# Attention and squared-ReLU MLP on one core: down products in halves, outputs half a chunk later, background steps interleaved, x loaded ahead

## The chip, the cores and the metric

The kernel runs on one core of one Trainium2 chip. The metric is the device time of one launch in microseconds (us). The kernel before took a median of 578.99 us over 3 runs (578.84, 578.99, 581.28). The profiled execution took 579.12 us; its span, from the first to the last instruction of the trace, is 577.3 us, so 1.8 us lie outside the span.

## The reference, cut to what matters

```python
x: (4, 12480, 128)   inducing: (32, 128)   w_in: (128, 2048)   w_out: (2048, 128)

def mab(q, kv):
    s = scale * (q @ kv.transpose(0, 2, 1))
    s = s - s.max(-1, keepdims=True)
    a = np.exp(s)
    a /= a.sum(-1, keepdims=True) + 1e-09
    return a @ kv
h = mab(I, x)               # 32 rows of summary per batch, over all 12480 tokens
y = mab(x, h)               # every token attends to the 32 rows
r = np.maximum(y @ w_in, 0.0)
out = (r * r) @ w_out
```

Four batches of 12480 tokens pass through two attentions and then through an MLP with squared ReLU. In the second attention each token's row is a mixture of only 32 rows of `h`, with weights `a`.

## The kernel before, in words

**What is computed instead of the wide MLP.** Since y = a·h, a hidden unit is a·(h·w_in). Where such a unit keeps its sign over all tokens, its squared ReLU is a quadratic form in the 32 weights. The kernel writes that form with squares of differences of two weights: one product with the constant 0/1/-1 matrix `pairs` gives 512 values per token (`hp`, four blocks of 128), their squares are `g`, and a product with 512x128 weights `w16` plus a product with `lin` gives the output (`po`). `w16`, `lin` and what scales them belong to a batch and are worked out from `h`, `w_in` and `w_out`. A few units without a fixed sign go through rows 96 to 127 of the input tile `dT` (`sq`, `z`, `zz`). A flag tells whether the form holds; the general path behind it (from `all_columns` on) is not executed here.

**Stages of a batch** b, with 26 chunks of 480 tokens (120 tokens of each of four quarters), in 7 groups G of four chunks, the last one of two:
- `first(b)`: per group, load x transposed (`xp`, 9 buffers), scores `s` on TensorE, scaling and row maximum into `sT` on VectorE (L254). Then the global maximum (`m1`, `mt`, `gm`, `mb`, `nb`), per group exp on ScalarE (L300), a transpose into `en` (L310), `largest(G)`: the largest |x| of the group in one pass over up to 1920 columns (`xm`, L292), and 15 products with rows of x (`xnb`, 5 buffers) that are added up in `hq` (`hacc`, L323 and L331). Then `hs`, `hn`, `ht` and `hT`, the transposed summary.
- `prepare(b)`: `hwv` = h·w_in (16 products; copied out of PSUM by `evac`, L163), the bounds (`am`, `bc`, `two`), `hws` and its f16 form `hw16` (L497), `hwS`, `R`, `pl`, `rb`, `cat`, `w4`, and four times a table `G` (L605) whose 16 products `wq` give a block of `w16` (L165).
- `second(b, G)`: the scores of the second attention, exp, division by the sum (GpSimd does the subtraction and the multiplication), a transpose, a split into two f16 parts `a16`, out to DRAM (`ad`) and back as rows 0 to 95 of `dT`.
- `squares(b, G)`: `sq` on TensorE, `z` on VectorE, `zz` on GpSimd, four DMAs into rows 96 to 127 of `dT`.

**The main loop** runs over 104 chunks in two halves j. In each half ScalarE squares two blocks of `hp` into `g` (`lift`, L648, `g` has 3 buffers), TensorE writes the two blocks of the next chunk (`up`, L639, two PSUM slots). In the first half TensorE also does all five products of the chunk before (`down`: four of L654 and one of L655, two PSUM slots), the output `o` is scaled by ScalarE (L658) or VectorE (L660, `o` has 3 buffers) and its DMA is issued. After that `background(k)` writes whatever steps of the other stages are due: `second` runs two to three groups ahead, `first` and `prepare` of the next batch are spread over the 26 chunks, and `squares` runs a group ahead.

**What sets the order.** The generators give the order in which the program is written, and a step is what lies between two `yield`s. A scheduler then orders each engine's instructions by its own estimates, with the order of writing as the priority; each engine executes its list in order. Which engine takes an `o` or the high part of `a16` is decided by `to_act` from running sums of estimates. All DMAs are issued by one queue, SP's, in one order; GpSimd issues none.

**Before the main loop** a prologue turns the 64-bit words of the weights into f32 on VectorE (`narrow`), with `first(0)` between (at the steps named in `WHEN`), then `prepare(0)`. The first `g` starts at 100.27 us.

## Time and profile before

| what | value |
|---|---|
| median of 3 runs | 578.99 us |
| profiled execution, its span | 579.12 us, 577.3 us |
| mean granted TensorE clock | 0.869 |
| TensorE busy | 438.9 us (76%) |
| VectorE busy | 365.3 us (63%) |
| ScalarE busy | 296.8 us (51%) |
| GpSimd busy | 83.4 us (14%) |
| first `g` of the four batches | 100.3, 236.7, 360.8, 486.6 us |
| busy share of the 16 DMA engines by the hardware queue | 52.1% |

The busy shares are means over stages with different limits; the views by window, by group of instructions and by wait are read for each stage. "Idle before" in a group is the time that its engine stood still directly before these instructions, with what ended most of it. PE is TensorE's matmuls, PEld its weight loads, DVE VectorE, ACT ScalarE, POOL GpSimd and SPq the queue that issues the DMAs.

### The profile page before, as it was taken

How to read it: one execution, taken by the hardware profiler on the slowest of the kernel's cores; microseconds unless marked ns; L12 is line 12 of the kernel's file. 1: busy time of each engine (PE TensorE's matmuls, PEld its weight loads, DVE VectorE, ACT ScalarE, POOL GpSimd, SP SyncE). 2: the span in 40 equal slices, each digit the busy share in tenths (PEclk: the TensorE clock that was granted, in tenths of full speed). 3: DMA queues.
4: the chain of work that ended last, by engine and by line, in shares of the span. 5: the costliest groups of instructions: out<-in, count | busy, mean ns of one | idle time of the engine just before them, and what ended most of it. 6: DMA issues, size and time to landing. Idle time of an engine off the chain costs nothing.

```text
span 577.3 us, 8820 instructions
## 1 busy us (share of the span) xinstructions
PE 438.9 (76%) x3083; PEld 204.5 (35%) x3083; DVE 365.3 (63%) x947; ACT 296.8 (51%) x419; POOL 83.4 (14%) x93
## 2 busy tenths in 40 slices
PE   1615465777798889769878899769777999897882
PEld 0014334522233536413333545313243555223330
DVE  6999758662555268997254298985534378767342
ACT  0030112437577266747875376628574476565771
POOL 0000011030211010242021021222011022422010
PEclk9999655997789569989889799969969599899997
DMA  8958715024528606565867535735866332334543
GB/s 322 399 214 277 277 69 154 1 86 155 179 80 305 199 20 226 172 182 167 280 226 230 178 102 186 270 104 145 311 211 190 107 105 72 97 126 130 168 132 131
DMA packets 64590, 100.82 MB, mean 175 GB/s; under 512 B 22800, under 2 KB 53776, under 8 KB 64528
## 3 DMA queue, kind: packets, MB, share of 16 engines
q1 hardware_dynamic: 64528, 100.08, 52.1%
q8 instruction: 28, 0.46, 0.3%
q14 instruction: 34, 0.28, 0.2%
HBM read 64.91 MB, written 31.95 MB: 168 GB/s over the span
## 4 chain that ended last, share of the span: by engine, by line
PE 44%; DVE 28%; ACT 13%; issue 6%; DMA 3%; POOL 3%; SPq 1%; POOLq 0%; ACTq 0%; DVEq 0%
PE po L654 10%; PE hp L639 9%; ACT g L648 8%; PE s L236 7%; DVE xm L292 5%; PE hwv L448 5%; PE hacc L323 4%; DVE G L605 3%; DMA outT_dram<-o 2%; PE po L655 2%; PE wq L611 2%; ACT o L658 2%; DVE e L362 2%; PE R L529 2%; DVE z L372 2%
## 5 line engine op out<-in xcount | busy, mean ns | idle before, releaser
L648 ACT ACTIVATE g<-hp 128x960 f16<-128x960 f32 x208 | 193.2, 970 | 87.9 <-PE hp L639 48.9
L639 PE MATMUL hp<-dT,pairs 96*128 96x480 f16 x416 | 122.0, 385 | 29.0 <-ACT g L648 28.1
L654 PE MATMUL po<-g,w 128*128 128x480 f16 x416 | 119.4, 399 | 16.1 <-ACT o L658 6.0
L368 POOL TENSOR_TENSOR e<-e,mx 128x480 f32<-128x480 f32 (+1 forms) x28 | 26.5, 947 | 334.8 <-DVE mx L364 222.8
L639 PEld LDWEIGHTS <-pairs 96*128 96x128 f16 x416 | 37.8, 99 | 97.6 <-issue 75.7
L654 PEld LDWEIGHTS <-w 128*128 128x128 f16 x416 | 41.1, 104 | 75.4 <-issue 43.9
L292 DVE TENSOR_REDUCE xm<-xp_False 128x1 f32<-128x1920 f32 (+1 forms) x28 | 55.7, 1989 | 5.3 <-DMA xp_False<-xT_dram 5.3
L658 ACT ACTIVATE o<-po,bias,osc 128x480 f32<-128x480 f32 x66 | 48.9, 753 | 18.9 <-PE po L655 7.1
L236 PE MATMUL s<-xp_False,indT_sb 128*32 128x480 f32 (+1 forms) x224 | 37.7, 743 | 20.5 <-DMA xp_False<-xT_dram 12.3
L323 PE MATMUL hacc<-xnb,en 128*32 128x128 f32 x784 | 39.2, 328 | 17.2 <-issue 9.3
L655 PE MATMUL po<-dT,lin 128*128 128x480 f16 x104 | 42.3, 408 | 2.7 <-DMA dT<-zz 2.7
L432 POOL TENSOR_TENSOR zz<-z 128x480 f16<-128x480 f32 (+1 forms) x28 | 28.9, 1030 | 87.8 <-DVE z L428 72.1
L660 DVE TENSOR_SCALAR o<-po,osc,bias 128x480 f32<-128x480 f32 x38 | 28.7, 767 | 18.0 <-DMA outT_dram<-o 6.8
L323 PEld LDWEIGHTS hacc<-xnb,en 128*32 128x32 f32 x784 | 26.7, 129 | 34.3 <-issue 20.1
L300 ACT ACTIVATE sT<-sT,nb 128x480 f32<-128x480 f32 (+1 forms) x28 | 18.2, 653 | 35.5 <-DVE nb L287 35.5
L236 PE MATMUL s<-xp_False,hT 128*32 128x480 f32 (+1 forms) x224 | 34.5, 628 | 2.1 <-DVE s L357 1.7
L375 POOL TENSOR_TENSOR e<-e,z 128x480 f32<-128x480 f32 (+1 forms) x28 | 27.6, 986 | 53.8 <-DVE z L374 48.6
L428 DVE TENSOR_SCALAR z<-sq,off,cut 128x480 f32<-128x480 f32 (+1 forms) x28 | 21.4, 764 | 21.8 <-PE sq L422 21.7
L605 DVE TENSOR_TENSOR G<-hwp,hw 128x512 f16<-128x512 f16 x64 | 30.1, 510 | 5.0 <-PE wq L611 4.7
L369 ACT ACTIVATE e<-e 128x480 f32<-128x480 f32 (+1 forms) x28 | 16.1, 574 | 31.6 <-POOL e L368 31.6
L362 DVE STREAM_TRANSPOSE e<-s 128x480 f32<-128x480 f32 (+1 forms) x28 | 18.0, 644 | 15.4 <-PE s L236 14.9
L331 DVE TENSOR_TENSOR hq<-hacc,hq 128x128 f32<-128x128 f32 x24 | 6.8, 284 | 33.0 <-PE hacc L323 33.0
(208 smaller groups left out, 498.6 us busy)
## 6 DMA issues: line engine op xcount, KB each, us to landing
outT_dram<-o SPq DMA_DIRECT2D x104, 240.0 KB, 2.2
xp_False<-xT_dram SPq DMA_DIRECT2D x24, 960.0 KB, 5.8
xnb<-xn_dram SPq DMA_DIRECT2D x28, 448.0 KB, 6.1
xnb<-xn_dram SPq DMA_DIRECT2D x24, 512.0 KB, 5.8
dT<-ad SPq DMA_DIRECT2D x72, 120.0 KB, 2.7
ad<-a SPq DMA_DIRECT2D x24, 240.0 KB, 2.7
dT<-zz SPq DMA_DIRECT2D x104, 30.0 KB, 1.9
wi<-w_in_dram SPq DMA_DIRECT2D x4, 512.0 KB, 5.4
```

Source lines behind the costliest of these rows:

```text
L236: nc.tensor.matmul(ps[32 * q:32 * q + 32, 0:w], lhsT, xp[:, w * q:w * q + w], start=True, stop=True,)
L292: nc.vector.tensor_reduce(st.xm[:, G:G + 1], st.xp[G], axis=AX.X, op=ALU.max, apply_absolute_value=True,)
L323: st.last = nc.tensor.matmul(hacc[32 * q:32 * q + 32, 0:P], en[:, t], xg[:, t % 8], start=t < 4, stop=t + 4 >= nb32,)
L362: nc.vector.transpose(ef[:, 0:wb], ps[:, 0:wb])
L432: nc.gpsimd.tensor_tensor(g[rows], zv[rows], zv[rows], op=ALU.mult)
L448: nc.tensor.matmul(ps[:, k * (MI + 1):(k + 1) * (MI + 1)], w_in_sb[:, f:f + P], st.hT[:, 96:P + 1], start=True, stop=True,)
L605: tt(g[:, :, MI * j:MI * j + n], hwp[:, :, 0:n], hw16f[:, :, s0:s0 + n], op=ALU.mult)
L639: nc.tensor.matmul(hp[:, i, 0:CH].rearrange("p (q t) -> p q t", q=4), pairs[0:96, (2 * j + i) * P:(2 * j + i + 1) * P], self.dT[0:96], sta ...
L648: nc.scalar.activation(self.g[:, 2 * j:2 * j + 2], self.hp.pop(j)[:, 0:2, 0:CH], AF.Square)
L654: nc.tensor.matmul(po[:, 0:CH], st.w16[:, i], self.g[:, i], start=i == 0, stop=False)
L655: nc.tensor.matmul(po[:, 0:CH].rearrange("p (q t) -> p q t", q=4), st.lin, self.dT, start=False, stop=True)
L658: nc.scalar.activation(o, po[:, 0:CH], AF.Identity, bias=st.bias, scale=st.osc)
```

## The change

What it does, part by part:

1. `down` takes a half: products 0 and 1 are written in the first half of the next chunk, products 2 and 3 and the one with `lin` in its second half. The output of chunk n-2 is written as a function of its own, `out`, after the first lift of chunk n; that is half a chunk later than before.
2. `background` returns the list of due steps instead of doing them; the lists of `second`, of the next batch and of `squares` are interleaved one by one, and every other step is written ahead of the down products, the rest behind. `second` has two more `yield`s (between the subtraction and exp, and behind the transpose `a32`), and the step counts follow it.
3. `first` asks for three groups of `xp` before it starts and for one more per group; two of the row blocks `xnb` are asked for at group 4, three at the last group; before, `xp` was asked for a step ahead of its group and all five `xnb` behind the last group. `WHEN` is (0, 2, 4, 8, 10, 11, 12).
4. `largest` takes half a group per pass; the transpose `en` and exp of the next group are written ahead of these passes.
5. The copies of `hwv`, the two f16 copies `hw16` and the scaling of `w16` go from ScalarE (in the case of `hwv` and `w16`: from the choice of `evac`, which the profile shows on ScalarE each time) to VectorE. `cs` is copied a step sooner, the two copies into `g4` are behind a `yield`.

All calls on TensorE, ScalarE and VectorE go through a wrapper (`pe`, `act`, `dve`) that changes nothing, since `KEPT` is empty; in the listings of the changed program these instructions all carry its line, L75. The diff without the lines that only take the wrapper's name:

```diff
-WHEN = (0, 2, 4, 8, 10, 12, 14)
+LEAD = 3
+KEPT = ()
+WHEN = (0, 2, 4, 8, 10, 11, 12)
...
-        one.xm = const.tile([P, NG], F32, name=f"xm{k}")
+        one.xm = const.tile([P, 2 * NG], F32, name=f"xm{k}")
...
-        for G, w in enumerate(WID):
-            if b:
-                st.xp[G] = load_xT(b, G)
-                yield
...
-        xns = {h: load_xn(h) for h in range(XB)}
+        if b:
+            for G in range(LEAD):
+                st.xp[G] = load_xT(b, G)
+            yield
+        xns = {}
+        for G, w in enumerate(WID):
+            if b and G + LEAD < NG:
+                st.xp[G + LEAD] = load_xT(b, G + LEAD)
+            if G == NG - LEAD or G == NG - 1:
+                for h in range(XB):
+                    if (h < 2) == (G < NG - 1):
+                        xns[h] = load_xn(h)
...
-        def largest(G):
-            held["dve"] += 60 + 1.042 * 4 * WID[G]
+        def largest(G, k):
+            held["dve"] += 60 + 1.042 * 2 * WID[G]
+            dve.tensor_reduce(
+                st.xm[:, 2 * G + k:2 * G + k + 1], st.xp[G][:, 2 * k * WID[G]:2 * (k + 1) * WID[G]], axis=AX.X, op=ALU.max,
+                apply_absolute_value=True,
...
+        ens = {0: turned(0)}
+        largest(0, 0)
+        yield
+        for G, nb32 in enumerate(BLK):
+            en = ens.pop(G)
...
+            else:
+                ens[G + 1] = turned(G + 1)
+            largest(G, 1)
+            if G + 1 < NG:
+                largest(G + 1, 0)
             yield
...
         nc.gpsimd.tensor_tensor(e[:, 0:t], e[:, 0:t], mx[:, 0:t].unsqueeze(2).broadcast_to([P, t, MI]), op=ALU.subtract)
+        yield
...
-            evac(hwv[:, 8 * h:8 * h + 8].rearrange("p k i -> p (k i)"), ps[:, 0:8 * (MI + 1)], 8 * (MI + 1))
+            dve.tensor_copy(hwv[:, 8 * h:8 * h + 8].rearrange("p k i -> p (k i)"), ps[:, 0:8 * (MI + 1)])
...
-            nc.scalar.copy(hw16[:, :, k], hws)
+            dve.tensor_copy(hw16[:, :, k], hws)
...
-            evac(st.w16[:, c], ps[:, 0:P], P, tsg[:, c:c + 1])
+            ts(st.w16[:, c], ps[:, 0:P], tsg[:, c:c + 1], None, op0=ALU.mult)
...
-        def down(self):
+        def down(self, part):
             st = self.st
+            if part == 0:
+                self.po = ps_o.tile([P, 512], F32, tag="po", name=f"po_{self.b}_{self.c}")
+            po = self.po
+            for i in (2 * part, 2 * part + 1):
+                pe.matmul(po[:, 0:CH], st.w16[:, i], self.g[:, i], start=i == 0, stop=False)
+            if part == 0:
+                return
+            pe.matmul(po[:, 0:CH].rearrange("p (q t) -> p q t", q=4), st.lin, self.dT, start=False, stop=True)
...
-    N_SECOND, N_SCORES, N_HEADS, N_PRE, N_SQ = 4, 2 * NG, 20, 23, 2
+    N_SECOND, N_SCORES, N_HEADS, N_PRE, N_SQ = 6, NG + 1, 14, 23, 2
...
+        steps = []
+        while any(lists):
+            steps += [one.pop(0) for one in lists if one]
+        return steps
...
+            k += 1
+            steps = background(k)
             chunk.lift(j)
+            if j == 0 and n > 1:
+                chunks[n - 2].out()
             if nxt:
                 nxt.up(j)
-            if j == 0 and n:
-                chunks[n - 1].down()
-            k += 1
-            background(k)
+            for gen in steps[0::2]:
+                next(gen, None)
+            if n:
+                chunks[n - 1].down(j)
+            for gen in steps[1::2]:
+                next(gen, None)
```

Three places show how the change moves instructions. The first is TensorE in the last batch, around the first block of chunk 13 (a row is the tile written, what it is made of, and its size; the weight loads between the products are left out). Before:

```order
2647 L639 MATMUL hp_13_0_5116<-dT_3_4884,pairs 128x480
...
2649 L654 MATMUL po_11_5119<-g_11_5086,w_1_146 128x480
...
2657 L655 MATMUL po_11_5119<-dT_2_4777,lin_147 128x480
...
2659 L639 MATMUL hp_13_1_5152<-dT_3_4884,pairs 128x480
...
2663 L639 MATMUL hp_14_0_5157<-dT_3_4884,pairs 128x480
```

With the change:

```order
2650 L75 MATMUL hp_13_0_5144<-dT_3_4903,pairs 128x480
...
2654 L75 MATMUL po_11_5164<-g_11_5113,w_1_146 128x480
...
2658 L75 MATMUL hp_13_1_5174<-dT_3_4903,pairs 128x480
...
2662 L75 MATMUL po_11_5164<-g_11_5113,w_1_146 128x480
...
2664 L75 MATMUL po_11_5164<-dT_2_4802,lin_147 128x480
...
2668 L75 MATMUL hp_14_0_5186<-dT_3_4903,pairs 128x480
```

Two of the five products of chunk 11 now stand ahead of the second block of chunk 13, three behind it.

The second is VectorE in the prologue, between the last `hq` of batch 0 and its `hn` (`xm_133` belongs to batch 0, `xm_144` to batch 1). Before:

```order
116 L333 TENSOR_REDUCE hq_317<-zs_314 128x1
117 L218 TENSOR_REDUCE wmax<-wm_170 128x1
118 L455 TENSOR_REDUCE xm<-xm_133 128x1
119 L244 MEMSET sT_890 128x16
120 L292 TENSOR_REDUCE xm_144<-xp_0_False 128x1
121 L338 TENSOR_SCALAR zr<-hs_502 128x1
122 L292 TENSOR_REDUCE xm_144<-xp_1_False 128x1
123 L339 RECIPROCAL zr<-zr 128x1
124 L340 TENSOR_SCALAR hn_134<-hs_502,zr 128x128
```

With the change:

```order
122 L75 TENSOR_REDUCE hq_317<-zs_314 128x1
123 L75 TENSOR_REDUCE xm_133<-xp_6_False 128x1
124 L75 TENSOR_SCALAR zr<-hs_509 128x1
125 L75 TENSOR_REDUCE wmax<-wm_170 128x1
126 L75 TENSOR_REDUCE xm<-xm_133 128x1
127 L75 RECIPROCAL zr<-zr 128x1
128 L75 MEMSET sT_897 128x16
129 L75 TENSOR_REDUCE xm_144<-xp_0_False 128x1
130 L75 TENSOR_SCALAR hn_134<-hs_509,zr 128x128
```

Two passes over whole groups of batch 1 stood ahead of `hn`; now it is one pass over half a group of batch 1, and one over half of batch 0's last, shorter group.

The third is VectorE in `prepare(1)`, behind `hws`. Before:

```order
340 L494 TENSOR_SCALAR hws_1695<-hwv_1581,s 128x512
341 L362 STREAM_TRANSPOSE e_1_0_1691<-s_1_0_1686 128x480
342 L506 TENSOR_TENSOR up_c<-up_c,vm 128x16
343 L509 TENSOR_SCALAR dn_c<-lo_c,two 128x16
344 L364 TENSOR_REDUCE mx_1_0_1693<-e_1_0_1691 128x15
345 L508 SCALAR_TENSOR_TENSOR dead<-up_c,nmg,dead 128x16
```

With the change:

```order
357 L75 TENSOR_SCALAR hws_1710<-hwv_1589,s 128x512
358 L75 STREAM_TRANSPOSE e_1_0_1696<-s_1_0_1691 128x480
359 L75 TENSOR_SCALAR z_5_1705<-sq_5_1700,off_137,cut 128x480
360 L75 TENSOR_REDUCE mx_1_0_1698<-e_1_0_1696 128x15
361 L75 CAST hw_1_1712<-hws_1710 128x16x32 x2
362 L75 TENSOR_TENSOR up_c<-up_c,vm 128x16
```

The two casts of `hws` are now in VectorE's list (a bare `hw_1` is the tile `hw16` of batch 1), and `z` of group 5 stands among these rows sooner than before.

More of the change, by code (lines that the diff above doesn't have):

```diff
@@ L427, in squares @@
         held["dve"] += 110 + 1.042 * CH
-        nc.vector.tensor_scalar(z[rows], ps[rows, 0:CH], st.off[rows], cut[rows], op0=ALU.add, op1=ALU.max)
+        dve.tensor_scalar(z[rows], ps[rows, 0:CH], st.off[rows], cut[rows], op0=ALU.add, op1=ALU.max)
         yield
@@ L481, in prepare @@
         ps = att_psum(f"bc_{b}")
-        nc.tensor.matmul(ps[:, 0:2], ones, row, start=True, stop=True)
+        pe.matmul(ps[:, 0:2], ones, row, start=True, stop=True)
         two = small("two", 2)
-        nc.vector.tensor_copy(two, ps[:, 0:2])
+        dve.tensor_copy(two, ps[:, 0:2])
         rho = two[:, 1:2]
@@ L707, in attend_then_relu2_mlp, with due, give @@
     given = {"ahead": 0, "sqs": 0, **{b: 0 for b in nexts}}
-    def give(what, gen, want):
-        while given[what] < want:
+    def due(what, gen, want):
+        steps = [gen] * max(0, want - given[what])
+        given[what] += len(steps)
+        return steps
+    def give(*args):
+        for gen in due(*args):
             next(gen, None)
-            given[what] += 1
     for n, _ in enumerate(prepare(0)):
@@ L723, in background @@
         b, c = k // (2 * NCH), k % (2 * NCH) / 2.0
-        give("ahead", ahead, min(math.ceil((NG * b + c / 4 + min(3, 2 + k / 16)) * N_SECOND), NB * NG * N_SECOND))
+        lists = [due("ahead", ahead, min(math.ceil((NG * b + c / 4 + min(3, 2 + k / 16)) * N_SECOND), NB * NG * N_SECOND))]
         if b + 1 < NB:
```

348 lines of the change are left out of this document (180 added, 168 removed).

## The prediction

> **What bounds the kernel now.** I read the page first: engine shares and the chain of work that ended last.
>
> ```profile
> PE 438.9 (76%) x3083; PEld 204.5 (35%) x3083; DVE 365.3 (63%) x947; ACT 296.8 (51%) x419; POOL 83.4 (14%) x93
> PE 44%; DVE 28%; ACT 13%; issue 6%; DMA 3%; POOL 3%; SPq 1%; POOLq 0%; ACTq 0%; DVEq 0%
> ```
>
> No engine is full; TensorE carries most of the chain, VectorE the next share. Which one bounds which stage is seen in the windows (columns: window and length, busy us and instructions of PE, PEld, DVE, ACT, POOL; then TensorE's granted clock, DMA share, GB/s).
>
> ```profile
> 0.00:60.00 60.00, 23.03 (x239) 10.61 (x239) 54.41 (x132) 5.94 (x15) 1.19 (x9) 1.00 0.82 303
> 60.00:100.30 40.30, 21.98 (x115) 15.60 (x115) 29.01 (x85) 6.72 (x11) 4.42 (x4) 0.53 0.47 161
> 100.30:236.70 136.40, 116.00 (x858) 54.74 (x856) 76.06 (x226) 79.86 (x117) 18.53 (x20) 0.85 0.43 138
> 236.70:360.80 124.10, 103.22 (x772) 47.97 (x771) 77.21 (x203) 79.42 (x113) 20.57 (x22) 0.90 0.61 194
> 360.80:486.60 125.80, 105.97 (x766) 49.35 (x765) 78.98 (x210) 73.10 (x104) 20.76 (x22) 0.86 0.53 171
> 486.60:577.30 90.70, 68.73 (x338) 26.28 (x337) 49.66 (x95) 51.76 (x62) 17.96 (x19) 0.92 0.40 128
> 236.70:261.10 24.40, 16.22 (x111) 5.53 (x111) 22.69 (x44) 13.92 (x20) 7.47 (x8) 0.88 0.61 193
> 362.00:386.50 24.50, 17.23 (x111) 5.79 (x111) 22.91 (x46) 10.84 (x15) 7.08 (x7) 0.83 0.56 178
> ```
>
> The prologue is VectorE's (54.41 of the first 60 us), then a chain of small steps (60 to 100 us, nothing full). The four long windows are the batches: TensorE is busy 76 to 85% of each. The last two rows are the starts of batches 1 and 2: for 24 us VectorE is busy 93%. So VectorE bounds the starts and TensorE's list the rest. The waits say how the main loop's two engines hold each other up (waiting engine, what it waits for: us in all, times, longest).
>
> ```profile
> ACT g L648 <- PE hp L639: 48.9, 43, 6.3
> ACT g L648 <- PE po L654: 32.5, 22, 3.8
> PE hp L639 <- ACT g L648: 28.1, 56, 2.8
> ```
>
> ScalarE waits 81.4 us (48.9 + 32.5) for TensorE. Of it, the waits for `hp` come where scores, `hacc` or a whole down product stand ahead of an `hp`; the waits for `po` come where `g` has no free buffer, because the products of the chunk three back are late.
>
> **Edit 1 and 2, halves and spread steps.** What can be won is part of those 81.4 us. The groups give a product's spacing:
>
> ```profile
> L639 PE MATMUL hp<-dT,pairs 96*128 96x480 f16 x416 | 122.0, 385 | 29.0 <-ACT g L648 28.1
> L654 PE MATMUL po<-g,w 128*128 128x480 f16 x416 | 119.4, 399 | 16.1 <-ACT o L658 6.0 <-DVE o L660 5.7 <-ACT g L648 2.8
> L655 PE MATMUL po<-dT,lin 128*128 128x480 f16 x104 | 42.3, 408 | 2.7 <-DMA dT<-zz 2.7
> L236 PE MATMUL s<-xp_False,indT_sb 128*32 128x480 f32 x192 | 35.1, 794 | 20.5 <-DMA xp_False<-xT_dram 12.3 <-DVE sT L254 4.7 <-DVE z L428 3.4
> L323 PE MATMUL hacc<-xnb,en 128*32 128x128 f32 x784 | 39.2, 328 | 17.2 <-issue 9.3 <-DVE en L310 5.7 <-DMA xnb<-xn_dram 1.0
> L448 PE MATMUL hwv<-hT,w_in_sb 128*128 128x33 f32 x128 | 26.3, 383 | 0.7 <-DVE hT L346 0.7
> L648 ACT ACTIVATE g<-hp 128x960 f16<-128x960 f32 x208 | 193.2, 970 | 87.9 <-PE hp L639 48.9 <-PE po L654 32.5 <-DMA dT<-ad 5.8
> ```
>
> Busy time over count is 0.293 us for an `hp` product, 0.287 for a `po`, 0.407 for `lin`, 0.183 for a score, 0.050 for `hacc`, 0.205 for `hwv`; the small ones likewise. With these I added up, in both orders of TensorE, the work from each `hp` pair to the next. What exceeds one lift (0.970 us) sums to 215.1 us before and 205.3 after: 9.8 us less, of which 4.7 in the last batch and 3.3 in batch 1. That is little, since the scheduler keeps the longest runs: the `hwv` products stay one unbroken block, only a chunk sooner, and runs of scores stay together. ScalarE's real waits are 81.4 of the 215.1, or 0.38, so I take 0.38 x 9.8 = **-3.7 us**; the ends are 0 (the waits move) and -9.8.
>
> The wait for `po` hardly changes: the `po` products that stand behind the `hp` of the chunk three later are 30 before and 29 after, because the second part now comes half a chunk later. In the last batch, every fourth chunk looks like this (start, busy, engine, line, operation, in brackets the idle time before and its releaser):
>
> ```profile
> 538.64 0.78 DVE L428 TENSOR_SCALAR z<-sq,off,cut 128x480 f32<-128x480 f32 x1 [3.10 <-PE sq L422]
> 539.33 1.45 DVE L660 TENSOR_SCALAR o<-po,osc,bias 128x480 f32<-128x480 f32 x2
> 540.15 0.97 PE L654 MATMUL po<-g,w 128*128 128x480 f16 x4 [0.16 <-DVE o L660]
> 541.22 2.70 ACT L648 ACTIVATE g<-hp 128x960 f16<-128x960 f32 x3 [1.84 <-PE po L654]
> 544.26 1.83 ACT L648 ACTIVATE g<-hp 128x960 f16<-128x960 f32 x2 [0.35 <-PE hp L639]
> 547.19 0.97 ACT L648 ACTIVATE g<-hp 128x960 f16<-128x960 f32 x1 [1.09 <-PE hp L639]
> ```
>
> VectorE stands 3.10 us at `z`, behind it two outputs wait, behind these the products, and ScalarE loses 1.84 us. In the changed order `sq` and two `hp` still stand ahead of two whole down products, so this wait stays. The 0.35 us wait, for an `hp` behind a whole down product, should go; the 1.09 may. These are inside the -3.7. What covers an output half a chunk later is the second `po` slot; without that cover it would cost TensorE one output (0.77 us, L660 below) per chunk in which it bites.
>
> **Edit 5, ScalarE's copies to VectorE, and edit 4, half passes.**
>
> ```profile
> L163 ACT COPY hwv<-hwv 128x264 f32<-128x264 f32 x8 | 3.0, 379 | 32.9 <-PE hwv L448 32.9
> L497 ACT CAST hw<-hws 128x512 f16<-128x512 f32 x8 | 4.5, 614 | 0.5 <-DVE hws L494 0.4
> L165 ACT ACTIVATE w<-wq,tsg 128x128 f16<-128x128 f32 x16 | 5.9, 368 | 12.4 <-PE wq L611 12.4
> L344 DVE COPY hT<-ht 128x128 f32<-128x128 f32 x4 | 1.2, 292 | 2.2 <-PE ht L343 2.2
> L340 DVE TENSOR_SCALAR hn<-hs,zr 128x128 f32<-128x128 f32 x4 | 1.4, 350 | 0.1
> L387 DVE TENSOR_SCALAR a<-a,lessen 128x480 f16<-128x480 f32 x8 | 3.7, 466 | 0.1
> L660 DVE TENSOR_SCALAR o<-po,osc,bias 128x480 f32<-128x480 f32 x38 | 28.7, 767 | 18.0 <-DMA outT_dram<-o 6.8 <-ACT g L648 5.8 <-PE po L655 2.8
> L658 ACT ACTIVATE o<-po,bias,osc 128x480 f32<-128x480 f32 x66 | 48.9, 753 | 18.9 <-PE po L655 7.1 <-issue 6.1 <-DMA outT_dram<-o 4.1
> L292 DVE TENSOR_REDUCE xm<-xp_False 128x1 f32<-128x1920 f32 x24 | 51.1, 2131 | 3.0 <-DMA xp_False<-xT_dram 3.0
> L292 DVE TENSOR_REDUCE xm<-xp_False 128x1 f32<-128x960 f32 x4 | 4.6, 1139 | 2.3 <-DMA xp_False<-xT_dram 2.3
> ```
>
> ScalarE gives up 13.4 us (3.0 + 4.5 + 5.9). On VectorE a copy of 264 columns out of PSUM lies between the 292 ns of 128 columns and the 767 ns of 480: 0.475 us by the line between them. The cast of 512 columns is nearest L387: 0.50 us. The scaling of 128 columns is nearest L340: 0.35 us. Sum: 8 x 0.475 + 8 x 0.50 + 16 x 0.35 = 13.4 us. The passes over |x| become 48 of 1.14 us and 8 of about 0.64 (on the line of the two rows), 59.8 us instead of 55.7: +4.1. Against this, 4 outputs and 2 high parts move to ScalarE: -4.0. VectorE gains 13.5 us in all, ScalarE loses 9.0. Where they fall decides:
>
> - Batch starts. Counted in the two orders of VectorE from the first `G` to `m1` of the batch after next, the work shrinks by 2.9 us (batch 1) and 2.7 (batch 2): one group's passes move to earlier, idler places, and one and five outputs leave; the scalings of `w16` are already counted. About 24 of the some 70 us of such a stretch are VectorE-bound, so I take 1 us each, **-2 us**; ends 0 and -5.6.
> - `hT` to `G` in batches 1 to 3: +2 x 0.475 + 2 x 0.50 + one half pass 1.14 = 3.1 us each, 9.3 in all, if all of it is on the path. But the main loop runs on meanwhile, and the copies no longer stand behind lifts of 0.97 us in ScalarE's list. I take 0.5 each: **+1.5 us**; ends 0 and +9.3.
>
> [...]
>
> **Prologue.**
>
> ```profile
> 62.53 0.15 DVE L333 TENSOR_REDUCE hq<-zs 128x1 f32<-128x7 f32 x1
> 62.75 2.13 DVE L292 TENSOR_REDUCE xm<-xp_False 128x1 f32<-128x1920 f32 x1
> 64.87 2.14 DVE L292 TENSOR_REDUCE xm<-xp_False 128x1 f32<-128x1920 f32 x1
> 67.11 0.35 DVE L340 TENSOR_SCALAR hn<-hs,zr 128x128 f32<-128x128 f32 x1
> 100.27 0.97 ACT L648 ACTIVATE g<-hp 128x960 f16<-128x960 f32 x1 [5.77 <-DMA dT<-ad]
> ```
>
> The two passes of 4.27 us ahead of `hn` become 1.14 + 0.64 us, 2.5 less on the chain that leads to the first `g`. The displaced passes go into later gaps of the window 60 to 100 us, where VectorE is busy 29.0 of 40.3; some delay will come of that. I take **-2 us**; ends -3.2 and +1 (one half pass on the way).
>
> **Edit 3, x sooner**, costs and brings nothing in my sum. Waits for x are 12.3 us at the scores and 1.0 at `hacc` (L236 and L323 above), of which the most lies in the prologue, whose loads are already issued first. The work that hides it is the main loop. The same DMAs are issued, some ahead of outputs on SP's queue, and the output buffers are the cover; if that is gone, an output waits (6.8 us so far, L660).
>
> **Sum.** -3.7 - 2 + 1.5 - 2 = -6.2 us. The profiled execution took 579.12 us (577.3 of span and 1.8 around it), so 572.9; the median of the runs is 0.1 us lower, so the forecast is **573 us**. From the favourable ends (-9.8 - 5.6 + 0 - 3.2) it would be 560.5, from the others (0 + 0 + 9.3 + 1) 589.4.
>
> **Rivals.** "Same" means within 0.5%, 576.1 to 581.9 us; the three runs lie within 0.4% of each other, so less can't be told from no change.
>
> *A, no effect (chance 0.18, about 579).* The scheduler restores nearly the old order and waits move from one place to the next. For it: 30 against 29 late `po`, and the 1.84 us wait that stays. Against it: 9.8 us less excess. Then -3.7 turns to 0, and -2 and +1.5 cancel: 577 to 579.
>
> *B, slower (0.28, about 587).* VectorE's list between `hT` and `G` is the path of the batch change: at the end of a batch, the next batch's `w16` must be ready. If the chain is late by the full 3.1 us in three batches, 9.3 us are lost, less some 2 of the prologue: about 586, or 588 if the prologue wins nothing. It decides as soon as the `wq` products of a batch are still running when its first down product is due. For it: `G` and `wq` stand in the chain of the profile with 3% and 2%. Against it: the waits for `hp`, those at the batch change among them, are 1.1 us on the mean (48.9 in 43), so there is little sign of such lateness so far.
>
> *C, much faster (0.14, about 560).* TensorE's clock. Long stretches ran at half clock:
>
> ```profile
> 60.70:98.20 37.50, 19.88 (x99) 14.10 (x100) 27.81 (x81) 6.69 (x10) 4.42 (x4) 0.50 0.45 157
> 378.10:388.30 10.20, 8.14 (x33) 1.60 (x32) 8.38 (x16) 2.47 (x3) 1.94 (x2) 0.50 0.23 62
> 388.30:398.30 10.00, 9.34 (x60) 3.38 (x53) 5.76 (x13) 7.04 (x9) 2.86 (x3) 1.00 0.39 138
> 449.80:463.40 13.60, 12.88 (x53) 7.12 (x53) 5.23 (x28) 6.63 (x10) 0.00 (x0) 0.50 0.18 56
> ```
>
> If the clock is only ever full or half, the batches' means (0.85, 0.90, 0.86, 0.92 above) make 2 x (0.15 x 136.4 + 0.10 x 124.1 + 0.14 x 125.8 + 0.08 x 90.7) = 115 us at half. If steadier work frees half of that, 57 us of work shrinks by half, and by TensorE's share of the chain (0.44) 12.6 us come off: 573 - 12.6 = 560. Against it: the row at 449.80 is half clock although TensorE is busy 12.88 of 13.60 us, in the block of `hwv`, which the change leaves whole. [...]
>
> **How the numbers follow.** Forecast (563 to 576.1) 0.40, C 0.14, A 0.18, B 0.28. Faster 0.40 + 0.14 = 0.54, same 0.18, slower 0.28. Cases of both signs hold most of the chance: the forecast's own range is 563 to 580, the whole one 553 (C with half as much again, 573 - 19 = 554) to 592 (the bad ends, 589.4, and some us more, since the two orders were counted without their waits).
>
> **What would show it.** In the profile after: the first `g` at about 98 us; ScalarE's waits for `hp` and `po` together near 76 us, with the 1.84 us wait of the last batch still there and the 0.35 gone; the `hwv` copy near 0.475 us, the cast near 0.50, the scaling near 0.35; VectorE near 379 us, ScalarE near 288; batch starts VectorE-bound for 23 rather than 24 us. A mean clock above 0.90 would speak for C. First `g` of a batch later relative to the batch before, with VectorE full between `hT` and `G`, would speak for B. My forecast is wrong if those waits fall by 20 us or more, or if the stretch from the first `g` of a batch to the next one's grows.

## The result: slower by 1.3%, not faster

The changed kernel took a median of 583.64 us over 4 runs (581.94 to 590.1), the kernel before on the same chip 578.91 us (577.42 to 581.28). The ratio is 1.0126 with a 95% interval of 1.0078 to 1.0174: slower by more than 0.5%. The forecast was 573 us and faster; the time lies inside the range (553 to 592), the direction was wrong. The profiled execution took 581.94 us with a span of 580.2 us. Here and below medians are over all runs of a kernel, while ratios and their intervals leave out runs in a slower state that some executions show, so the two can differ.

The page of the changed kernel, engine shares and chain, answers to the first lines of the prediction:

```profile
PE 440.1 (76%) x3083; PEld 207.6 (36%) x3083; DVE 374.5 (65%) x1001; ACT 286.7 (49%) x393; POOL 82.4 (14%) x93
PE 46%; DVE 27%; ACT 8%; issue 7%; DMA 6%; POOL 3%; SPq 1%; POOLq 0%; ACTq 0%; DVEq 0%
```

VectorE (374.5 us against 379 forecast) and ScalarE (286.7 against 288) carry about the work that was worked out. The engines did what was expected of them; the time went elsewhere. The windows, cut at the first `g` of each batch (columns as in the prediction):

```profile
60.00:94.50 34.50, 21.87 (x114) 15.38 (x113) 28.14 (x91) 4.31 (x5) 4.25 (x4) 0.53 0.42 148
94.50:233.30 138.80, 113.04 (x854) 55.96 (x853) 83.46 (x249) 76.12 (x108) 19.03 (x20) 0.88 0.46 149
233.30:360.50 127.20, 108.01 (x770) 49.14 (x770) 76.54 (x213) 77.45 (x109) 20.11 (x21) 0.87 0.58 182
360.50:483.40 122.90, 103.47 (x778) 48.16 (x779) 81.81 (x220) 72.02 (x101) 20.38 (x21) 0.88 0.56 174
483.40:580.20 96.80, 71.05 (x333) 27.05 (x330) 49.83 (x95) 50.88 (x60) 17.44 (x18) 0.88 0.37 119
```

Against 40.3, 136.4, 124.1, 125.8 and 90.7 us before, that is -5.8 in the prologue, +2.4, +3.1 and -2.9 in batches 0 to 2, and +6.1 in batch 3, in which no next batch is prepared. Together that is +2.9 us, the difference of the spans (580.2 - 577.3). The waits of the main loop:

```profile
ACT g L75 <- PE po L75: 80.8, 20, 12.9
ACT g L75 <- PE hp L75: 55.9, 42, 5.2
PE hp L75 <- ACT g L75: 22.6, 41, 1.8
DVE hwv L75 <- PE hwv L75: 22.5, 8, 3.0
PE po L75 <- DVE o L75: 11.2, 7, 3.5
```

ScalarE's waits for `hp` and `po` are 136.7 us, where about 76 was forecast. Part of that is a change of name: before, ScalarE waited 32.9 us at the copies of `hwv`, which now are VectorE's, so it waits through the `hwv` block at the next lift instead (in the three batches that prepare another, waits of 12.87, 11.35 and 9.60 us, 33.8 us in all, have the `hwv` block in them). The forecast did not allow for that. The other 47 us of the waits for `po` stand against 32.5 before. TensorE's wait for an output on VectorE (`PE po <- DVE o`), 5.7 us before, doubled to 11.2. The stretches of batches 0 and 1 grew, which the prediction had named as a sign that it is wrong.

### The profile page after: what moved, and what is told of

It is laid out like the page before. It is cut to its first block, busy times and chain, and to the rows that moved or that the text cites. A ratio compares the mean times of both kernels' runs of the same rounds, so it can differ in the third digit from the quotient of the medians.

```text
span 580.2 us, 8833 instructions
## 1 busy us (share of the span) xinstructions
PE 440.1 (76%) x3083; PEld 207.6 (36%) x3083; DVE 374.5 (65%) x1001; ACT 286.7 (49%) x393; POOL 82.4 (14%) x93
## 4 chain that ended last, share of the span: by engine, by line
PE 46%; DVE 27%; ACT 8%; issue 7%; DMA 6%; POOL 3%; SPq 1%; POOLq 0%; ACTq 0%; DVEq 0%
PE po L75 15%; PE s L75 7%; PE hp L75 7%; ACT g L75 6%; PE hwv L75 5%; DVE z L75 4%; PE hacc L75 4%; DVE xm L75 4%; DVE a L75 3%; DVE G L75 3%; DMA xp_False<-xT_dram 3%; PE wq L75 3%; PE R L75 2%; POOL e L412 2%; ACT o L75 1%
## 5 line engine op out<-in xcount | busy, mean ns | idle before, releaser
L75 ACT ACTIVATE g<-hp 128x960 f16<-128x960 f32 x208 | 194.1, 969 | 137.6 <-PE po L75 80.8
L75 PE MATMUL po<-g,w 128*128 128x480 f16 x416 | 132.0, 410 | 20.4 <-DVE o L75 11.2
L75 PE MATMUL hp<-dT,pairs 96*128 96x480 f16 x416 | 123.9, 376 | 25.4 <-ACT g L75 22.6
L75 PEld LDWEIGHTS <-w 128*128 128x128 f16 x416 | 41.7, 106 | 79.6 <-issue 51.0
L75 PEld LDWEIGHTS <-pairs 96*128 96x128 f16 x416 | 38.5, 99 | 85.9 <-issue 61.1
L75 ACT ACTIVATE o<-po,bias,osc 128x480 f32<-128x480 f32 x70 | 51.2, 748 | 19.0 <-PE po L75 7.6
L75 DVE TENSOR_REDUCE xm<-xp_False 128x1 f32<-128x960 f32 (+1 forms) x56 | 59.4, 1063 | 1.0 <-DMA xp_False<-xT_dram 1.0
L75 PE MATMUL s<-xp_False,indT_sb 128*32 128x480 f32 (+1 forms) x224 | 36.3, 723 | 22.4 <-DMA xp_False<-xT_dram 12.0
L75 PE MATMUL hacc<-xnb,en 128*32 128x128 f32 x784 | 39.5, 326 | 17.3 <-issue 13.3
L75 PE MATMUL po<-dT,lin 128*128 128x480 f16 x104 | 42.5, 411 | 0.5 <-DMA dT<-zz 0.5
L75 PEld LDWEIGHTS hacc<-xnb,en 128*32 128x32 f32 x784 | 26.7, 128 | 36.7 <-issue 28.5
L75 DVE TENSOR_TENSOR hq<-hacc,hq 128x128 f32<-128x128 f32 x24 | 6.8, 285 | 49.5 <-PE hacc L75 49.5
L75 PE MATMUL s<-xp_False,hT 128*32 128x480 f32 (+1 forms) x224 | 35.6, 639 | 1.6 <-DVE s L75 1.5
L75 ACT ACTIVATE sT<-sT,nb 128x480 f32<-128x480 f32 (+1 forms) x28 | 18.3, 654 | 33.8 <-DVE nb L75 33.8
L75 DVE TENSOR_SCALAR o<-po,osc,bias 128x480 f32<-128x480 f32 x34 | 25.6, 766 | 12.3 <-PE po L75 10.6
L75 DVE TENSOR_SCALAR z<-sq,off,cut 128x480 f32<-128x480 f32 (+1 forms) x28 | 21.1, 755 | 16.4 <-PE sq L75 16.3
L75 ACT ACTIVATE e<-e 128x480 f32<-128x480 f32 (+1 forms) x28 | 16.1, 575 | 25.9 <-POOL e L404 25.9
L75 DVE TENSOR_TENSOR G<-hwp,hw 128x512 f16<-128x512 f16 x64 | 28.6, 501 | 0.0
L75 PEld LDWEIGHTS hwv<-hT,w_in_sb 128*128 128x128 f32 x128 | 26.4, 317 | 3.9 <-PE ht L75 2.4
```

Source lines behind the costliest of these rows:

```text
L75: ins = getattr(self.engine, op)(*args, **kwargs)
```

## Which part does it: each undone alone

Theory before the runs ("late release"): the second half of the products and the output come half a chunk later, `g` and the `po` slots come free later. Rivals: the copies on VectorE; the steps written ahead of the down products ("interleaving"). The runs are compared by their ratio to the kernel before on the same chip, which took 576.9 to 578.6 us (median) in the five studies.

**Run u_halves**, all five products and the output in the first half of the next chunk:

```diff
-            if j == 0 and n > 1:
-                chunks[n - 2].out()
...
-            if n:
-                chunks[n - 1].down(j)
+            if j == 0 and n:
+                chunks[n - 1].down(0)
+                chunks[n - 1].down(1)
+                chunks[n - 1].out()
```

> The changed kernel with part 1 undone: all five products of a chunk and its output are written in the first half of the next chunk, everything else as changed. Theory 'late release': the second half of the products and the output come half a chunk later, so g and the po slots come free later; ScalarE's waits for po (80.8 us against 32.5) are the loss, above all in batch 3 (96.8 us against 90.7). Then this run is 5 us or more faster than the changed kernel (578 or less), and batch 3 is back near 91. Rival 'copies': the halves cost nothing, the copies on VectorE do; then within 2 us of the changed kernel, 582 to 585. Rival 'interleaving': the steps written ahead of the down products hold them up; then the products are late here too, and the time stays above 581.

Measured: 576.39 us, ratio 1.0023 (0.9941 to 1.0106). The profiled execution took 580.62 us, the longest of the ten. In it batch 3 stayed at 96.9 us, and two lines of its waits read

```profile
ACT g L75 <- PE hp L75: 68.5, 49, 8.5
ACT g L75 <- PE po L75: 67.6, 21, 10.0
```

By the centres some 1% comes back, though the interval overlaps that of the changed kernel, and not where the theory put it: in this long execution the waits of 136.1 us in all (136.7 in the changed kernel) only moved from `po` to `hp`.

**Run u_steps**, no interleaving, all due steps behind the down products:

```diff
-        while any(lists):
-            steps += [one.pop(0) for one in lists if one]
-        return steps
+        return [step for one in lists for step in one]
...
-            for gen in steps[0::2]:
-                next(gen, None)
             if n:
                 chunks[n - 1].down(j)
-            for gen in steps[1::2]:
+            for gen in steps:
                 next(gen, None)
```

> The changed kernel with part 2 undone: no interleaving, all due steps are written behind the down products, list by list (the two added yields stay). Theory 'late release': the second half and the output are still late, little changes, within 2 us of the changed kernel. Rival 'interleaving': 5 us or more faster, 578 or less, with the waits of ScalarE for po below 50 us. Rival 'copies': no change.

Measured: 567.27 us (561.13 to 568.15), ratio 0.9893 (0.975 to 1.0036). The interval reaches 1, but it does not touch that of the changed kernel (1.0078 to 1.0174). This is the largest step of the four, and it is the rival's, except that the waits for `po` were 59.9 us where it expected less than 50. The halves are still in it, so lateness by halves alone is not the cause.

**Run u_copies**, the copies back on ScalarE:

```diff
-            dve.tensor_copy(hw16[:, :, k], hws)
+            act.copy(hw16[:, :, k], hws)
...
-            ts(st.w16[:, c], ps[:, 0:P], tsg[:, c:c + 1], None, op0=ALU.mult)
+            act.mul(st.w16[:, c], ps[:, 0:P], tsg[:, c:c + 1])
```

and the copies of `hwv` in the same way.

> The changed kernel with the copies of hwv, the casts of hw16 and the scaling of w16 back on ScalarE. Theory 'late release': no more than 2 us of difference. Rival 'copies': VectorE gets 16.0 us back (3.5 + 6.9 + 5.6 by the profile of the changed kernel), of which at least 5 show: 578 or less, and hT to the first G is shorter in each batch. Rival 'interleaving': no change.

Measured: 581.19 us, ratio 1.0145 (1.001 to 1.0281), no different from the changed kernel. The first `g` was at 97.7 us instead of 94.5, and the waits for `po` went back to 32.2 us, with 66.9 us at the `hwv` copies in their place: the change of name, seen from the other side.

**Run u_passes**, one pass over a group, ahead of the products with x, and the weights' steps (`WHEN`) and the step count at their old values (the main hunk):

```diff
-            else:
-                ens[G + 1] = turned(G + 1)
-            largest(G, 1)
-            if G + 1 < NG:
-                largest(G + 1, 0)
             yield
+            if G + 1 < NG:
+                ens[G + 1] = turned(G + 1)
+                largest(G + 1)
+                yield
```

> The changed kernel with part 4 undone: the largest |x| in one pass over a group again, written ahead of the products with x as before, and the steps of the weights at their old places. All theories expect the prologue's gain of 5.7 us (first g at 94.5 us instead of 100.3) to go for the most part, if the shorter passes made it: first g at 98 or later and the time 3 us or more above the changed kernel, 586 or more. If the first g stays near 95, another part made that gain.

Measured: 585.18 us, ratio 1.0236 (1.0124 to 1.0348), first `g` at 101.7 us. Without this part the prologue's gain is gone.

**Runs again, u_behind, u_lists, u_yields.** The interleaving is two things: steps ahead of the products, and lists mixed one by one. The second study separates them, with the changed kernel itself beside it, and takes out the added yields.

> The changed kernel itself once more, so that the runs that undo a part are compared with it on one chip. All theories: 580 to 586 us, 1 to 1.5% above the kernel before.

> The changed kernel with the steps still interleaved one by one, but all of them behind the down products. The run with both taken back was 567 us. Theory 'ahead of the products': it is the steps written ahead of the down products that make the products late; then 570 or less, as that run. Rival 'round robin': it is the interleaving of the lists, which pulls the next batch's and the squares' steps ahead of the second attention's; then no better than the changed kernel, 580 or more.

> The counterpart: lists one behind the other as before, but every other step still ahead of the down products. Theory 'ahead of the products': as slow as the changed kernel, 580 or more. Rival 'round robin': 570 or less.

> The changed kernel without the two yields added in the second attention (four steps per group again). Batch 3 took 94.5 to 97 us in the changed kernel and in all four runs that undid one part, 90.7 before. If the added yields, which spread a group's second attention over more half chunks, make that, batch 3 is back at 92 or less here and the time 4 us or more below the changed kernel. If batch 3 stays above 94, the cause is elsewhere (the halves together with the interleaving, or the order in which x was asked for).

u_behind has only the second hunk of u_steps, u_lists only the first, and u_yields is

```diff
         nc.gpsimd.tensor_tensor(e[:, 0:t], ..., op=ALU.subtract)
-        yield
         act.activation(e[:, 0:t], e[:, 0:t], AF.Exp, scale=scale)
...
         dve.transpose(a[:, 0:wb], ef[:, 0:wb])
-        yield
...
-    N_SECOND, ... = 6, ...
+    N_SECOND, ... = 4, ...
```

| run | median us | ratio to before (95%) |
|---|---|---|
| again (the changed kernel) | 587.99 | 1.0133 (1.0048 to 1.0218) |
| u_behind | 568.46 | 0.9834 (0.9774 to 0.9893) |
| u_lists | 575.66 | 0.9953 (0.9911 to 0.9995) |
| u_yields | 587.54 | 1.015 (1.0087 to 1.0213) |

Putting the same steps behind the down products takes 3.0% off (1.0133 to 0.9834, about 17 us); mixing the lists costs too (1.0133 to 0.9953), but only with steps ahead: u_steps and u_behind, without and with mixing, have medians of 567.3 and 568.5. u_lists lies between what both of its theories expected (580 or more, 570 or less): with unmixed lists the steps ahead cost less, 0.9953 against 0.9893 in u_steps with overlapping intervals. The yields are neutral in this surrounding: batch 3 stayed at 97.3 us. The theory of late release by halves falls.

## The steps ahead of the products: alone, and what they hold up

**Run p_ahead** adds this one thing to the kernel before, with the down product whole and the lists one behind the other (`background` returns the list here too):

```diff
-            if j == 0 and n:
-                chunks[n - 1].down()
             k += 1
-            background(k)
+            steps = background(k)
+            for gen in steps[0::2]:
+                next(gen, None)
+            if j == 0 and n:
+                chunks[n - 1].down()
+            for gen in steps[1::2]:
+                next(gen, None)
```

> The kernel before with one thing added: of the due steps, list by list as before, every other one is written ahead of the down product of that half, the rest behind. Theory 'ahead of the products': slower than the kernel before by 4 us or more, 582 or above, with ScalarE's waits for po well above 32.5 us. Rival 'only with halves': within 2 us of the kernel before, since the down product is whole and stands in every other half only.

Measured: a median of 588.46 us (582.14 to 596.21), the kernel before 576.92 beside it (571.71 to 585.57). These runs scatter too much for an interval. Two of the four, 582.14 and 582.66, can be compared with ten of the kernel before (571.71 to 579.84, mean 576.3): 6 us more, 1.1%. So it costs alone too, though less than in the changed kernel; ScalarE's waits for `po` are 43.8 us instead of 32.5. The windows of its batches:

```profile
100.40:232.80 132.40, 108.27 (x845) 49.54 (x844) 74.40 (x222) 79.17 (x114) 16.91 (x18) 0.91 0.45 146
232.80:359.20 126.40, 98.70 (x775) 44.51 (x773) 77.40 (x201) 80.18 (x116) 19.80 (x21) 0.93 0.59 190
359.20:482.80 123.60, 99.70 (x779) 45.88 (x777) 80.63 (x210) 73.36 (x105) 21.47 (x23) 0.89 0.54 171
482.80:580.40 97.60, 68.17 (x342) 26.46 (x340) 53.22 (x100) 51.48 (x62) 18.55 (x19) 0.91 0.38 119
```

The four together are 3.0 us longer than before (480.0 against 477.0), although TensorE's busy time fell from 393.9 to 374.8 us: what TensorE stands still grew by 22 us. The loss is in batch 3 (97.6 against 90.7); batches 0 to 2 together are 3.9 us shorter. The profile shows two ways in which the steps cost. VectorE's and TensorE's rows in batch 3 (start, busy, engine, line, operation, idle time before with its releaser):

```profile
501.76 0.68 DVE L388 SCALAR_TENSOR_TENSOR a<-a,lessen,a 128x480 f16<-128x480 f32 x1
503.32 0.68 DVE L378 STREAM_TRANSPOSE a<-e 128x480 f32<-128x480 f32 x1 [0.89 <-POOL e L375]
504.03 0.47 DVE L387 TENSOR_SCALAR a<-a,lessen 128x480 f16<-128x480 f32 x1
504.42 0.77 DVE L428 TENSOR_SCALAR z<-sq,off,cut 128x480 f32<-128x480 f32 x1
505.11 1.45 DVE L660 TENSOR_SCALAR o<-po,osc,bias 128x480 f32<-128x480 f32 x2
505.93 1.76 PE L654 MATMUL po<-g,w 128*128 128x480 f16 x4 [5.99 <-DVE o L660]
508.52 0.97 ACT L648 ACTIVATE g<-hp 128x960 f16<-128x960 f32 x1 [7.72 <-PE hp L639]
```

Steps of the second attention and a `z` now stand ahead of two outputs in VectorE's list. Most of the time VectorE works on them; one waits 0.89 us for GpSimd. Both `po` slots hold finished products; TensorE stands 5.99 us at the next `po`, behind it the `hp`, and ScalarE loses 7.72 us. And on TensorE, in batch 2:

```profile
378.75 0.59 PE L422 MATMUL sq<-dT,singles 96*32 96x480 f16 x4 [4.39 <-DMA dT<-ad]
385.25 1.83 PE L236 MATMUL s<-xp_False,indT_sb 128*32 128x480 f32 x8 [3.79 <-DVE z L428]
387.01 0.58 PE L655 MATMUL po<-dT,lin 128*128 128x480 f16 x1
387.56 1.43 PE L236 MATMUL s<-xp_False,indT_sb 128*32 128x480 f32 x8
388.92 0.58 PE L639 MATMUL hp<-dT,pairs 96*128 96x480 f16 x2
389.60 0.97 ACT L648 ACTIVATE g<-hp 128x960 f16<-128x960 f32 x1 [10.95 <-PE hp L639]
```

`sq`, which waits 4.39 us for a DMA, and scores that wait 3.79 us until VectorE has done its `z` stand ahead of the products and of `hp`: 10.95 us of ScalarE. (Batch 2 as a whole got no longer by it, 123.6 us against 125.8.) The changed kernel has the pattern of the first rows in batch 3:

```profile
513.61 1.32 DVE L75 SCALAR_TENSOR_TENSOR a<-a,lessen,a 128x480 f16<-128x480 f32 x1
514.85 0.67 DVE L75 STREAM_TRANSPOSE e<-s 128x480 f32<-128x480 f32 x1
515.45 1.41 DVE L75 TENSOR_SCALAR o<-po,osc,bias 128x480 f32<-128x480 f32 x2
516.24 1.76 PE L75 MATMUL po<-g,w 128*128 128x480 f16 x4 [3.45 <-DVE o L75]
518.09 0.97 ACT L75 ACTIVATE g<-hp 128x960 f16<-128x960 f32 x1 [6.87 <-PE po L75]
```

Here VectorE does not wait; its work on the steps alone makes the two outputs late. So in these rows a step holds up what is written behind it on its engine, by its own work (TensorE's 3.45 us here) and by what it waits for (the 4.39 and 3.79 us in p_ahead); no run separates the two.

With the steps behind, the windows of u_behind are

```profile
93.30:222.50 129.20, 108.69 (x855) 53.36 (x855) 82.46 (x250) 75.86 (x107) 19.24 (x21) 0.92 0.50 161
222.50:347.60 125.10, 104.76 (x772) 47.82 (x771) 76.04 (x213) 77.77 (x110) 21.12 (x22) 0.88 0.59 185
347.60:468.90 121.30, 104.03 (x781) 49.06 (x779) 79.58 (x222) 72.26 (x100) 22.30 (x22) 0.89 0.56 174
468.90:561.50 92.60, 69.04 (x330) 26.35 (x327) 48.88 (x94) 51.46 (x60) 17.17 (x18) 0.91 0.40 125
```

so 9.6, 2.1, 1.6 and 4.2 us less than in the changed kernel, 17.5 in all. TensorE's busy time for nearly as many products (2738 against 2735) is 9.0 us of that (386.5 against 395.6); the other half is time in which it stood still. The busy part shows where the orders are alike: around `R` of batch 1 the same 32 products took 6.20 us in the one and 3.68 in the other.

```profile
210.21 6.20 PE L75 MATMUL R<-wo_sb,hwS 128*32 128x128 f32 x32 [1.00 <-DVE hwS L75]
```

```profile
201.80 3.68 PE L75 MATMUL R<-wo_sb,hwS 128*32 128x128 f32 x32 [0.40 <-DVE hwS L75]
```

The first row is the changed kernel's, the second u_behind's. The wait ahead of the block is 1.00 against 0.40 us. The windows of the four chunks around it, 20 to 23 of batch 0, have a granted clock of 0.84 and of 1.00:

```profile
203.90:225.50 21.60, 19.33 (x135) 12.05 (x134) 17.08 (x56) 12.36 (x18) 2.69 (x3) 0.84 0.45 149
```

```profile
196.50:215.40 18.90, 16.64 (x134) 10.34 (x133) 16.61 (x55) 12.42 (x18) 3.02 (x3) 1.00 0.52 170
```

Whether the longer waits brought the clock down was not tried by itself and stays open. By the sums above about half of the 17.5 us would be the clock's at most (an estimate), and in p_ahead the steps cost time although its clock was no lower than before but in batch 3 (0.91, 0.93, 0.89, 0.91 against 0.85, 0.90, 0.86, 0.92).

## Without the steps ahead it is faster than before: which part makes that

**Runs c_behind_whole and c_behind_copies** start from u_behind and undo the halves, or put the copies back on ScalarE, with the hunks shown above.

> The changed kernel with all steps behind the down products (568 us that way) and, besides, the down product whole with its output at once, as before. Theory 'one bad pair': halves are harmless or good once no step stands ahead of them; then this is no faster than 568, rather 570 to 575. Rival 'late release': the halves cost on their own (undoing them in the changed kernel gave some 7 us); then 564 or less.

> The changed kernel with all steps behind the down products, and the copies of hwv, hw16 and w16 back on ScalarE. If the copies on VectorE are good or neutral: 568 or more, up to 574, with ScalarE waiting at its hwv copies for 30 us or more. Rival 'copies cost': 563 or less.

Measured: 566.76 us, ratio 0.9791 (0.9683 to 0.9899), and 567.93 us, ratio 0.9851 (0.978 to 0.9921); u_behind had 0.9834. The first lies between what the two theories expected (568 or more, 564 or less). Neither the halves nor the copies make a difference clear of noise once the steps stand behind.

**Runs p_passes and p_x** add one part to the kernel before: the half passes (the hunk of u_passes taken the other way), or x asked for sooner (the hunk with `LEAD` in the diff of the change, `N_SCORES = NG + 1`). Both also have the changed places of `cs`, of `g4` and of `m1` (the maximum over the groups, which the change takes into the last score step).

> The kernel before with part 4 alone (two passes for the largest |x|, the transpose and exp of the next group ahead of them, the places of the weights' steps that go with it; also cs and the copies into g4 at their changed places). If the prologue's gain is this part's: first g at 96 us or sooner instead of 100.3, and the time 3 to 6 us below the kernel before. If it needs the copies on VectorE or x sooner: first g at 98 or later and no change.

> The kernel before with x asked for sooner and nothing else but the places of cs and of the copies into g4. If x sooner makes the gain on its own: 572 or less. If it is worth nothing alone: 575 to 581, as the kernel before.

Measured: p_passes 578.48 us, ratio 1.0033 (0.9982 to 1.0085), nothing, with the first `g` at 99.4 us; p_x **564.3 us** (562.59 to 566.98), ratio **0.9764 (0.9721 to 0.9807)**, the lowest median and ratio of all, though its interval overlaps those of most runs with the steps behind. Its windows from the first `g` on, and the row of `nb` for batch 1 in the kernel before and then in p_x:

```profile
100.90:226.20 125.30, 107.94 (x858) 51.95 (x856) 76.82 (x227) 79.23 (x117) 18.55 (x20) 0.93 0.50 159
226.20:351.60 125.40, 105.62 (x771) 48.31 (x770) 74.76 (x199) 80.64 (x117) 20.21 (x22) 0.88 0.59 184
351.60:472.70 121.10, 101.11 (x766) 46.07 (x766) 77.98 (x209) 73.82 (x105) 21.12 (x22) 0.90 0.56 179
472.70:565.10 92.40, 67.27 (x338) 26.34 (x337) 48.42 (x93) 52.80 (x64) 17.85 (x19) 0.93 0.39 126
```

```profile
168.27 0.12 DVE L287 TENSOR_SCALAR nb<-mb 128x1 f32<-128x1 f32 x1
```

```profile
155.60 0.11 DVE L75 TENSOR_SCALAR nb<-mb 128x1 f32<-128x1 f32 x1
```

`nb` closes the score stage; exp and `hacc` follow. With x sooner it comes at chunk 10.5 of batch 0 instead of 14, and likewise in batches 1 and 2 (9.5 and 10 instead of 13.5 and 14). The products with x, which end ahead of `hT` at chunk 19 in both, then spread over some nine chunks instead of five. Batch 0 shrinks by 11.1 us (136.4 to 125.3) and batch 2 by 4.7; batches 1 and 3 grow by 1.3 and 1.7. The waits for x that the profile had shown were small; what the earlier loads changed is the order: the program writes the step of `nb` a little behind chunk 8 in both, and the scheduler places it three and a half to four chunks sooner.

That this earlier place makes the gain is not shown, and other runs don't bear it out. The changed kernel has `nb` at chunks 11, 10.5 and 10.5 and is slower than before; of the runs below, c_behind_passes has it at 11, 9.5 and 10 and gains nothing, c_behind_x at 12.5, 13 and 12.5 and gains 1.6%. In p_x itself batch 1 grows with an equally early `nb`. In its profile TensorE's busy time in the four windows is 12.0 us less than before for as many products (381.9 against 393.9), nearly all of the 12.8 us by which they shrink, at clocks of 0.93, 0.88, 0.90 and 0.93 against 0.85, 0.90, 0.86 and 0.92. So x sooner was worth 13 us here; by which way stays open.

**Runs c_behind_x, c_behind_passes, c_behind_yields** take one part out of u_behind.

> The changed kernel with all steps behind the down products (568 us), and x asked for as before. If x sooner makes the gain over the kernel before: 574 or more. The prediction had it at nothing: then within 2 us of 568.

> The changed kernel with all steps behind the down products, and the largest |x| in one pass as before. If the prologue's gain comes through: first g at 100 us or later and 573 to 576 (5 to 7 us slower than 568). If other stages take it up: within 3 us of 568.

> The changed kernel with all steps behind the down products, without the two yields added in the second attention. If the yields make the gain: 574 or more. If they are neutral, as they were in the changed kernel: 566 to 570.

| run | median us | ratio to before (95%) |
|---|---|---|
| c_behind_x | 568.85 | 0.9843 (0.9799 to 0.9888) |
| c_behind_passes | 579.92 | 1.0045 (1.0007 to 1.0083) |
| c_behind_yields | 570.96 | 0.9832 (0.9784 to 0.9881) |

The parts don't add up. x sooner is worth 13 us alone and nothing here; the half passes are worth nothing alone and 2% here, part of it in the prologue (first `g` at 101.6 us against 93.3).

Read in pairs, the runs of the two surroundings take the same step, the steps from ahead of the products to behind them, six times:

| besides | steps ahead | steps behind |
|---|---|---|
| nothing (again, u_behind) | 1.0133 (1.0048 to 1.0218) | 0.9834 (0.9774 to 0.9893) |
| no added yields (u_yields, c_behind_yields) | 1.015 (1.0087 to 1.0213) | 0.9832 (0.9784 to 0.9881) |
| copies on ScalarE (u_copies, c_behind_copies) | 1.0145 (1.001 to 1.0281) | 0.9851 (0.978 to 0.9921) |
| no halves (u_halves, c_behind_whole) | 1.0023 (0.9941 to 1.0106) | 0.9791 (0.9683 to 0.9899) |
| whole passes (u_passes, c_behind_passes) | 1.0236 (1.0124 to 1.0348) | 1.0045 (1.0007 to 1.0083) |
| lists not mixed (u_lists, u_steps) | 0.9953 (0.9911 to 0.9995) | 0.9893 (0.975 to 1.0036) |

Each ratio is to the kernel before on the same chip. With mixed lists the steps ahead cost 1.9 to 3.2% each time, with intervals that don't overlap; without mixing the difference is not clear.

**Runs p_x_passes and p_x_passes_copies** add the half passes, and then the copies, to p_x.

> The kernel before with x sooner (564 us alone) and the half passes with the places of the weights' steps. If the passes matter because they free VectorE's list for the copies moved there, they bring little here: 562 to 566. If they help whenever x comes sooner: 560 or less, with the first g at 99 us or sooner.

> The same with the copies of hwv, hw16 and w16 on VectorE besides. The prologue should gain some 4 us (first g at 95 or sooner, as in all runs with both). If that comes through: 2 us or more below the run without the copies. If the batches lose it again on VectorE: no faster than that run, 562 or more.

Measured: 570.39 us (562.4 to 577.14; the scatter allows no interval, and only the runs of 562.4 and 568.56 can be compared) and 568.99 us, ratio 0.9873 (0.9825 to 0.992). Nothing came on top: the passes bring little, as the first expectation's first branch had it, and the run with the copies is no faster. The first `g` was at 99.9 and 99.3 us; the 95 that was expected of passes and copies together failed. With both but without the added yields it is also at 98.3 (u_yields) and 99.2 (c_behind_yields), without the copies at 97.7 (u_copies) and 98.1 (c_behind_copies), so the early first `g` takes all three: passes, copies and yields. Why whole passes cost in u_behind and not beside x sooner alone stays open; all these orders come from the same scheduler, and each part moves the places of the others.

## Why the prediction was wrong, step by step

- **Edit 1 and 2, -3.7 us: failed.** This is the step that turned the sign. Halves and spread steps were one term, sized by TensorE's own work between one `hp` and the next. That sum leaves out what the steps written ahead of the down products do on the other engines: VectorE's work on them stands ahead of the outputs that free the `po` slots, and some wait for GpSimd or a DMA (0.89 and 4.39 us in the rows of p_ahead). This is passed on to the products: TensorE stood 5.99 us at a `po` there. Steps ahead cost about 17 us in the changed kernel (again against u_behind) and 6 alone (p_ahead); the halves cost at most some 1% beside them and nothing that could be measured without them. What spoke for rival A, 30 against 29 late `po`, misled in the same way: the counts were the same, not what stands ahead of what.
- **The unchanged 1.84 us wait of batch 3: it grew.** It was found in the right place, two outputs behind a step of VectorE, and priced at what it was. In the changed kernel it reads (ScalarE, batch 3):

```profile
529.77 1.83 ACT L75 ACTIVATE g<-hp 128x960 f16<-128x960 f32 x2 [5.37 <-PE po L75]
542.05 1.83 ACT L75 ACTIVATE g<-hp 128x960 f16<-128x960 f32 x2 [3.50 <-PE po L75]
552.49 7.22 ACT L75 ACTIVATE g<-hp 128x960 f16<-128x960 f32 x8 [2.71 <-PE po L75]
562.47 2.69 ACT L75 ACTIVATE g<-hp 128x960 f16<-128x960 f32 x3 [2.76 <-PE po L75]
```

An output half a chunk later was priced as covered by the second `po` slot; here that cover was gone, and at 516.24 above TensorE waited 3.45 us for an output. p_ahead, whose outputs are not written later, has such a wait too (5.99 us), so the steps ahead are enough to take the cover away, without the half chunk.
- **Edit 3, nothing: right beside the other parts, wrong alone.** The waits for x (12.3 and 1.0 us) were read as the worth of asking sooner. With the steps behind, taking it out changes nothing (c_behind_x); in the changed kernel itself it was not taken out alone. On the kernel before it is worth 13 us, for a reason that stays open.
- **Edit 5, +1.5 us: nearly right.** The copies are neutral within the noise (u_copies, c_behind_copies). `hwv` took 433 ns (475 forecast), `w16` 348 (350). The casts took 905 ns instead of 500: see below. The two engines differ both ways at the copies out of PSUM: `hwv` took 433 ns on VectorE and 379 on ScalarE, `w16` 348 on VectorE and 368 on ScalarE.
- **Batch starts, -2 us:** no run measures this term by itself, and it stays open.
- **Prologue, -2 us: mis-sized.** It gained 5.8 (first `g` at 94.5, forecast about 98). The shorter passes ahead of `hn` are only half of it: `hn` starts at 64.16 us instead of 67.11. `two`, further down the chain, starts at 80.92 instead of 85.79, with half a pass ahead of it instead of a whole one, and without the copies or the yields the first `g` comes 3 to 4 us later.
- **Rival B, slower, 0.28:** it held the sign and 587 us, but its mechanism, VectorE between `hT` and `G` at the batch change, is not it: the copies put back change nothing that could be measured. **Rival C:** the clock did not rise: 0.88, 0.87, 0.88 and 0.88 in the batches against 0.85, 0.90, 0.86 and 0.92. Its 12.6 us rest on the author's estimate that steadier work frees half of the time at half clock; no run shows that term.

## What to carry to other kernels

Writing background steps ahead of the products that free a buffer is not spreading them: the work of such a step on VectorE or TensorE, and what it waits for, held up the release of the buffer here (TensorE stood 5.99 us at a `po` in p_ahead, 3.45 us in the changed kernel), so such steps belong behind. A sum of one engine's work over its order says nothing of this; look, for each instruction that frees a slot, at what now stands ahead of it, on its own engine too. Where a scheduler places the work, parts of a change don't add up: loading x sooner was worth 13 us alone and nothing beside the other parts, the half passes the reverse. So price parts by runs, one at a time and in the surrounding in which they will stand. x sooner alone, on the kernel before, gives the lowest median of this study, 564.3 us, 2.4% below the kernel before and 3.3% below the median of the changed kernel, which ran on another chip.
